# Batch 0's scores in two halves of the tokens, and the order of the transposes of the next batch's x

## The chip, the cores and the metric

The kernel runs on one core of a Trainium2 chip. The metric is the device time of one execution, in microseconds; lower is better.

## The reference, cut to what matters

```python
B, H, S, Ns, D = (8, 8, 512, 32, 64)          # x: B H S D, state: B H Ns D
# attention in both directions
scores  = scale * x @ state.T                  # per head, S x Ns
a       = softmax(scores)                      # over the 32 states
xread   = a @ state
scores2 = scale * state @ x.T                  # per head, Ns x S
a2      = softmax(scores2)                     # over the 512 tokens
sread   = a2 @ x
x2      = concat([xread, sread], axis=2)       # B H (512+32) D -> 4352 x 512
# two linear layers
h   = x2 @ w_in                                # 512 -> 2048
g   = h * sigmoid(1.702 * h)
out = g @ w_out                                # 2048 -> 512, float32
```

The two weights come as float64; the kernel reads their 32-bit words and puts float32 together itself.

## The kernel before, in words

Everything is written out by hand: there is no scheduler, and each engine runs its instructions in the order in which the program issues them. The kernel handles the 8 batches one after another. For a batch it transposes the state (`att_state`, L252, copied from PSUM by ScalarE at L254) and x in four pieces of two heads (`att_xT`, L262, copied at L263), forms the scores with the matmuls of `by_state` (L280), takes both softmaxes, multiplies the state into `w_in` (`att_M`, L280 again, copied at L391), and runs the up product on the attention weights and that product, then Gelu, then the down product with `w_out`. Batches 0 and 1 use plain matmuls (L462 up, L480 down). From batch 2 on the up product is a Strassen scheme (`up_strassen`, L891, additions on VectorE at L901, Gelus on ScalarE at L898) and the down product a two-level one (`strassen_two`, L646) with seven block products P1 to P7; P1, for one, consists of two halves of 16 matmul records, P1a and P1b. Behind each half stands a hook: a list of steps of the next batch, made by `hooks_next`, that is issued there. The first hook, P1a, begins with the last steps of the up product (`rest`: two products, their additions and Gelus).

PSUM tiles come from pools that hand out their buffers in turn; a tile waits until the buffer's previous tile has been read. `att_ps` draws from `psA` with two buffers (tag "att"), and holds the transposes; `psH` has two buffers as well (tag "h") and holds up products; `bank_o` are four fixed banks.

```python
psA = ctx.enter_context(tc.tile_pool(name="psA", bufs=2, space=bass.MemoryType.PSUM))
psH = ctx.enter_context(tc.tile_pool(name="psH", bufs=2, space=bass.MemoryType.PSUM))
```

At the start, weights arrive in pieces of 512 KB through SyncE's one DMA queue: the first piece of `w_in`, then the state and the four token chunks of batch 0's x, then three more pieces of `w_in`, then batch 1's. A piece is rounded in two steps. `round_a` makes a mask: one operation on VectorE (L189) and two on ScalarE (L194, L195). `round_b` needs that mask and takes four operations on VectorE (L204 to L207). `powers_to(n)` issues the masks of the pieces below n, `round_to(n, ahead)` rounds the pieces below n, with masks some pieces ahead.

Batch 0's x is transposed by chunk of 128 tokens as it arrives (`att_xT_arriving`, L272, copied at L273 by VectorE and ScalarE in turn). Then come in program order: the scores of batch 0 over all 512 tokens (`att_scores`), the mask of the second piece, the 32x32 transposes of the scores on VectorE (`att_blocks`, L293), maximum, subtraction and exponential (`att_x_exp`, L329 to L331), the rounding of the second piece, the rest of that softmax (`att_x_norm`, L338 to L343), then batch 1's state, x and scores, the rounding of pieces 3 and 4, and `att_M(0, 0)`, the first use of rounded weights. `keep_warm(n)` puts n bfloat16 matmuls on zeros (L122) into TensorE's queue; their results aren't used.

Of the kernel before, what the change touches and what calls it, by code (L numbers as in the profile page):

```python
# [10 lines left out]
FP32 = mybir.dt.float32  # L11
I32 = mybir.dt.int32
U32 = mybir.dt.uint32
AF = mybir.ActivationFunctionType
ALU = mybir.AluOpType
AX = mybir.AxisListType
# [4 lines left out]
def kernel(  # L21
# [30 lines left out]
    nc = tc.nc  # L52

    B, H, S, D = x.shape
    Ns = state.shape[2]
    DM = H * D
    DF = moe_w_in.shape[1]
    P = 128
    NPR = P // Ns
    NG = H // NPR  # L60
    NF = DF // P
    SCH = S // P
# [3 lines left out]
    NB = S // Ns  # L66
    HF, HN = NF // 2, DM // 2
    scale = float(1.0 / np.sqrt(D))
# [10 lines left out]
    apool = ctx.enter_context(tc.tile_pool(name="apool", bufs=1))  # L79
# [4 lines left out]
    psH = ctx.enter_context(tc.tile_pool(name="psH", bufs=2, space=bass.MemoryType.PSUM))  # L84
# [4 lines left out]
    def att_ps(shape, name):  # L89
        return psA.tile(shape, FP32, tag="att", name=name)  # L90
# [26 lines left out]
    bank_o = [psO.tile([P, FC], FP32, tag=f"o{i}", name=f"o_{i}") for i in range(4)]  # L117

    def keep_warm(n):
        ps = psH.tile([P, FC], FP32, tag="h", name="warm")  # L120
        for _ in range(n):
            nc.tensor.matmul(ps, zeros[:, :P], zeros, start=True, stop=True)  # L122
# [17 lines left out]
    def x_heads(b, c, j):  # L140
        return xn[b][:, c, NG * j : NG * (j + 1)].rearrange("q g d -> q (g d)")
# [33 lines left out]
    for i, v in enumerate((8.0 * most, 8.0 * (most - least))):  # L175
        t = konst.tile([P, 1], FP32, name=f"edge_{i}")
# [7 lines left out]
    def round_a(i):  # L184

        _, hi = words(i)
        sc = low[:, 2 + i % (AHEAD + 1)].bitcast(I32)
        power[i] = sc
        nc.vector.tensor_scalar(sc, hi, 0x7FF00000, None, ALU.bitwise_and)  # L189
        if PIECES[i][0] == "o":  # L190
            nc.vector.tensor_scalar(sc, sc, most, least, ALU.min, ALU.max)
            nc.vector.tensor_scalar(sc, sc, -least, 8.0, ALU.add, ALU.mult)
            return
        nc.scalar.activation(out=sc.bitcast(FP32), in_=sc, func=AF.Relu, bias=edge[0], scale=-8.0)  # L194
        nc.scalar.activation(out=sc, in_=sc.bitcast(FP32), func=AF.Relu, bias=edge[1], scale=-1.0)  # L195
# [21 lines left out]
    def load_weights(upto):  # L217
        while done["load"] < min(upto, len(PIECES)):
            load_weight(done["load"])
            done["load"] += 1  # L220

    def powers_to(n):
        while done["a"] < min(n, len(PIECES)):
            load_weights(done["a"] + 1)
            round_a(done["a"])
            done["a"] += 1
# [21 lines left out]
    A = {b: {} for b in range(B)}  # L248
# [4 lines left out]
        A[b]["stT"] = apool.tile([P, P], FP32, tag="stT", name=f"stT_{b}", bufs=2)  # L253
        nc.scalar.copy(A[b]["stT"], ps)  # L254

    def att_xT(b, j, spare=False):
        if j == 0:
            A[b]["xT"] = apool.tile([P, NPR, S], FP32, tag="xT", name=f"xT_{b}")
        name = f"xT_{b}_{j}"
        ps = psH.tile([P, SCH, P], FP32, tag="h", name=name) if spare else att_ps([P, SCH, P], name)  # L260
        for c in range(SCH):
            nc.tensor.transpose(ps[:, c], x_heads(b, c, j), ident)  # L262
        nc.scalar.copy(A[b]["xT"][:, j], ps.rearrange("p c q -> p (c q)"))  # L263

    def att_xT_arriving(b, warm):

        A[b]["xT"] = apool.tile([P, NPR, S], FP32, tag="xT", name=f"xT_{b}")
        for c in range(SCH):
            keep_warm(warm)
            ps = att_ps([P, NPR, P], f"xT_{b}_{c}")  # L270
            for j in range(NPR):
                nc.tensor.transpose(ps[:, j], x_heads(b, c, j), ident)  # L272
            (nc.scalar.copy if c % 2 else nc.vector.tensor_copy)(A[b]["xT"][:, :, P * c : P * (c + 1)], ps)  # L273

    def by_state(b, ps, rhs):

        for j in range(NPR):
            for g in range(NG):
                rows, st = slice(D * g, D * (g + 1)), slice(Ns * j, Ns * (j + 1))
                nc.tensor.matmul(ps[g][st], A[b]["stT"][rows, st], rhs(rows, j), start=True, stop=True)  # L280

    def att_scores(b):
        a = A[b]
        a["s"] = bank_o[:NG] if b == 0 else bank_o[NG:]
        by_state(b, a["s"], lambda rows, j: a["xT"][rows, j])

    def att_blocks(b):

        a = A[b]
        t = apool.tile([P, NG, NB, Ns], FP32, tag="e1", name=f"e1_{b}")  # L290
        a["e1"] = t
        for g in range(NG):
            nc.vector.transpose(t[:, g].rearrange("p i n -> p (i n)"), a["s"][g])  # L293
# [30 lines left out]
    def att_x_exp(b):  # L324

        a = A[b]
        t = a["e1"].rearrange("p g i n -> p (g i) n")
        mx = apool.tile([P, NS1], FP32, tag="mx", name=f"mx_{b}")
        nc.vector.reduce_max(out=mx, in_=t, axis=AX.X)  # L329
        nc.vector.tensor_tensor(out=t, in0=t, in1=mx.to_broadcast((P, NS1, Ns)), op=ALU.subtract)  # L330
        nc.scalar.activation(out=t, in_=t, func=AF.Exp, scale=scale)  # L331
# [410 lines left out]
    def hooks_next(b):  # L742

        h = {}

        def at(name, fn, *args):
            h.setdefault(name, []).append((fn, args))

        at("P1a", att_state, b)
        at("P1a", att_xT, b, 0)  # L750
        at("P1b", att_xT, b, 1)
        at("P1b", att_xT, b, 2)
        at("P1b", att_xT, b, 3, True)
        at("P2a", att_scores, b)
        at("P2a", att_M, b, 0)
        at("P2a", att_M, b, 1, True)
        at("P2a", att_blocks, b)
        at("P2a", att_s_max, b)
        at("P2a", att_s_exp, b)
        for g in range(NG):  # L760
            at("P2a", x_max, b, g)
            at("P2a", x_sub, b, g)
        at("P2a", x_exp, b)
        at("P2", att_s_norm, b)
        for name, fn, *args in (
            ("P6.1", x_sum, 0), ("P6.2", x_sum, 1), ("P6.3", x_inverse), ("P6.4", x_scale, 0), ("P6.6", x_scale, 1),
        ):
            at(name, fn, b, *args)
        for g in range(NG):
            at("P6", att_eT, b, g)  # L770
            at("P6", x_back, b, g)
        at("P4a", att_sread, b)
        at("P4a", att_M, b, 3, True)
        at("P4a", att_M, b, 2)
        steps = up_sums(b)
        for name, n in (("P4b", 5), ("P7.1", 2), ("P7.2", 1), ("P7.3", 1), ("P7.4", 1), ("P7.6", 1), ("P7", 1), ("P3a", 3)):
            for fn, args in steps[:n]:
                at(name, fn, *args)
            steps = steps[n:]
        assert not steps  # L780
        at("P3a", att_srT, b)
        return h


    def up_sums(b):

        a = A[b]

        def tt(out, x0, x1, op=ALU.subtract):
            nc.vector.tensor_tensor(out=out(), in0=x0(), in1=x1(), op=op)  # L790

        def rooms(step):
            if step == 0:
                t = apool.tile([P, NG, NB, Ns], FP32, tag="e1", name=f"ta_{b}").rearrange("p g i n -> p (g i n)")
                a["T"] = [t[:, QT * i : QT * (i + 1)] for i in range(4)]
            elif step == 1:
                t = apool.tile([P, NPR, S], FP32, tag="xT", name=f"ms_{b}")
                a["S1"], a["S2"] = t[:, :2], t[:, 2:]
            else:
                t = apool.tile([P, NG, SCH, P], FP32, tag="eT", name=f"m4_{b}")  # L800
                a["S4"] = t.rearrange("p g c q -> p g (c q)")

        def T(i):
            return lambda: a["T"][i]

        def R(g, i):
            return lambda: a["aT"][:, g, QT * i : QT * (i + 1)]

        def M(c, g):
            return lambda: a["M", c][:, g]  # L810

        def V(name, c):
            return lambda: a[name][:, c]

        steps = [(rooms, (0,))]
        steps += [(tt, v) for v in ((T(0), R(0, 1), R(0, 0)), (T(1), R(1, 1), T(0)), (T(2), R(1, 1), R(0, 1)), (T(3), R(1, 0), T(1)))]
        steps.append((rooms, (1,)))
        for c in range(2):
            steps.append((tt, (V("S1", c), M(2 + c, 0), M(2 + c, 1), ALU.add)))
            steps.append((tt, (V("S2", c), V("S1", c), M(c, 0))))  # L820
            steps.append((tt, (M(2 + c, 0), M(c, 0), M(2 + c, 0))))
        steps.append((rooms, (2,)))
        steps += [(tt, (V("S4", c), M(c, 1), V("S2", c))) for c in range(2)]
        return steps
# [137 lines left out]
    round_to(1, 0)  # L962
    att_state(0)
    att_xT_arriving(0, 2)
    att_scores(0)
    powers_to(2)
    att_blocks(0)
    att_x_exp(0)
    round_to(2, 1)
    att_x_norm(0)  # L970
    keep_warm(24)
# [2 lines left out]
        keep_warm(2)  # L974
        att_xT(1, j)
    att_scores(1)
    keep_warm(24)
    powers_to(4)
    round_to(NPR, 2)
    att_M(0, 0)  # L980
# [142 lines left out]
```

## Time and profile before

| | |
|---|---|
| median of 3 runs | 747.09 us (745.83, 747.09, 747.61) |
| the profiled execution: its own time, its span | 747.61 us, 745.8 us |
| mean granted TensorE clock | 0.996 |
| TensorE matmul busy | 732.2 us (98%) |
| VectorE, ScalarE busy | 501.9 us (67%), 231.6 us (31%) |
| first M of batch 0 on TensorE | at 29.16 us |
| time from batch to batch at the hook P1a (state transposes at 246.62, 326.71, 406.81) | 80.1 us |

The span goes from the first to the last instruction of the profiled execution. PE is TensorE's matmuls, PEld its weight loads, DVE VectorE, ACT ScalarE, SP the engine that issues the DMAs. A line of a timeline gives start and duration in us, the engine, the line of the kernel and the operation, out<-in with tile names, shape and number of instructions, and in brackets the idle time of the engine before it and what ended that. A matmul in float32 is recorded as two.

### The profile page before, as it was taken

How to read it: one execution, taken by the hardware profiler on the slowest of the kernel's cores; microseconds unless marked ns; L12 is line 12 of the kernel's file. 1: busy time of each engine (PE TensorE's matmuls, PEld its weight loads, DVE VectorE, ACT ScalarE, POOL GpSimd, SP SyncE). 2: the span in 40 equal slices, each digit the busy share in tenths (PEclk: the TensorE clock that was granted, in tenths of full speed). 3: DMA queues.
4: the chain of work that ended last, by engine and by line, in shares of the span. 5: the costliest groups of instructions: out<-in, count | busy, mean ns of one | idle time of the engine just before them, and what ended most of it. 6: DMA issues, size and time to landing. Idle time of an engine off the chain costs nothing.

```text
span 745.8 us, 10913 instructions
## 1 busy us (share of the span) xinstructions
PE 732.2 (98%) x4553; PEld 568.0 (76%) x4555; DVE 501.9 (67%) x947; ACT 231.6 (31%) x421; POOL 0.8 (0%) x8
## 2 busy tenths in 40 slices
PE   8989999999999999999999999999999999999996
PEld 3423444458788798888888789878888888899995
DVE  5999699705946776576756765677657774768340
ACT  4667610121424411443134421451143313300220
POOL 0000000000000000000000000000000000000000
PEclk9999999999999999999999999999999999999999
DMA  9811246010012000300040003100030001000000
GB/s 234 337 58 56 85 142 173 0 54 3 29 46 45 1 15 30 74 1 15 2 102 1 15 2 83 21 1 16 29 74 1 15 2 42 1 15 29 15 1 28
DMA packets 48768, 35.29 MB, mean 47 GB/s; under 512 B 36432, under 2 KB 44112, under 8 KB 48720
## 3 DMA queue, kind: packets, MB, share of 16 engines
q1 hardware_dynamic: 48720, 34.61, 16.2%
q8 instruction: 35, 0.57, 0.3%
q14 instruction: 13, 0.11, 0.0%
HBM read 25.69 MB, written 8.91 MB: 46 GB/s over the span
## 4 chain that ended last, share of the span: by engine, by line
PE 95%; SPq 2%; DMA 1%; ACT 1%; issue 0%; DVE 0%; DVEq 0%; ACTq 0%
PE o L646 28%; PE o L891 16%; PE o L523 9%; PE h L462 8%; PE o L480 7%; PE low L598 6%; PE upx L891 6%; PE o L598 4%; PE M L280 4%; PE xT L262 2%; SPq L138 1%; PE sr L411 1%; PE o L280 1%; PE upx_sr L891 1%; DMA out_dram<-osb_sr 1%; PE warm L122 1%
## 5 line engine op out<-in xcount | busy, mean ns | idle before, releaser
L901 DVE TENSOR_TENSOR g<-o,g 128x512 f32<-128x512 f32 (+1 forms) x140 | 88.1, 651 | 87.4 <-PE o L891 86.3
L646 PE MATMUL o<-w_out,g 128*128 128x256 f32 x576 | 130.0, 380 | 0.0
L646 PEld LDWEIGHTS o<-w_out,g 128*128 128x128 f32 x576 | 107.4, 190 | 18.1 <-issue 4.2
L898 ACT ACTIVATE g<-g 128x512 f32<-128x512 f32 (+1 forms) x84 | 49.8, 599 | 100.5 <-DVE g L901 100.5
L891 PE MATMUL upx<-aT,M 128*128 128x256 f32 x192 | 49.3, 379 | 0.0
L891 PE MATMUL o<-ta,M 128*128 128x256 f32 x192 | 49.3, 379 | 0.0
L891 PE MATMUL o<-ta,ms 128*128 128x256 f32 x192 | 48.4, 380 | 0.0
L391 ACT COPY M<-M 128x512 f32<-128x512 f32 x64 | 33.2, 596 | 42.3 <-PE M L280 42.3
L646 PE MATMUL o<-sums,g 128*128 128x256 f32 x192 | 43.8, 382 | 0.0
L523 PE MATMUL o<-w_out,g 128*128 128x256 f32 x192 | 42.9, 380 | 0.0
L646 PE MATMUL o<-sums,later 128*128 128x256 f32 x192 | 42.4, 379 | 0.0
L646 PEld LDWEIGHTS o<-sums,g 128*128 128x128 f32 x192 | 35.6, 190 | 8.6 <-issue 4.2
L523 PEld LDWEIGHTS o<-w_out,g 128*128 128x128 f32 x192 | 36.1, 190 | 6.0 <-issue 1.3
L891 PEld LDWEIGHTS o<-ta,ms 128*128 128x128 f32 x192 | 36.4, 190 | 5.2 <-DVE osb L542 0.3
L891 PEld LDWEIGHTS upx<-aT,M 128*128 128x128 f32 x192 | 36.5, 190 | 5.0
L646 PEld LDWEIGHTS o<-sums,later 128*128 128x128 f32 x192 | 36.5, 190 | 5.0
L891 PEld LDWEIGHTS o<-ta,M 128*128 128x128 f32 x192 | 36.5, 190 | 5.0
L503 DVE TENSOR_TENSOR later<-g,g 128x512 f32<-128x512 f32 (+1 forms) x32 | 20.8, 650 | 21.5 <-ACT g L465 21.5
L462 PE MATMUL h<-low,M 128*128 128x512 f32 x64 | 31.5, 630 | 2.1 <-ACT M L391 2.1
L280 PE MATMUL M<-w_in,stT 64*32 64x512 f32 x512 | 33.2, 594 | 0.2 <-ACT eT L401 0.2
L462 PE MATMUL h<-aT,M 128*128 128x512 f32 x64 | 28.7, 599 | 2.3 <-ACT M L391 2.3
L601 DVE TENSOR_TENSOR pu<-low,pu 128x128 f32<-128x128 f32 x12 | 3.5, 291 | 39.6 <-PE low L598 39.6
(172 smaller groups left out, 1135.5 us busy)
## 6 DMA issues: line engine op xcount, KB each, us to landing
later<-in_moe_w_out_dram SPq DMA_DIRECT2D x16, 512.0 KB
xn<-in_x_dram SPq DMA_DIRECT2D x28, 256.0 KB
w_out<-in_moe_w_in_dram SPq DMA_DIRECT2D x12, 512.0 KB
out_dram<-osb SPq DMA_DIRECT2D x20, 256.0 KB
out_dram<-later SPq DMA_DIRECT2D x12, 256.0 KB
later<-in_moe_w_in_dram SPq DMA_DIRECT2D x4, 512.0 KB
sums<-in_x_dram SPq DMA_DIRECT2D x4, 256.0 KB
stn<-in_state_dram SPq DMA_DIRECT2D x16, 32.0 KB
```

The costliest lines, as they stand in the source:

```text
L262: nc.tensor.transpose(ps[:, c], x_heads(b, c, j), ident)
L280: nc.tensor.matmul(ps[g][st], A[b]["stT"][rows, st], rhs(rows, j), start=True, stop=True)
L391: nc.scalar.copy(m[:, g], ps[g])
L462: nc.tensor.matmul(hps, lhs[i], rhs[i], start=(i == 0), stop=(i == n - 1))
L480: nc.tensor.matmul(ops, G[key, f // 2][:, f % 2, P * r : P * (r + 1)], w_out[:, f], start=(f == 0), stop=(f == NF - 1))
L503: nc.vector.tensor_tensor(out=s1, in0=a21, in1=a22, op=ALU.add)
L523: nc.tensor.matmul(ps[:, r], lhs[f][:, P * r : P * (r + 1)], rhs[:, f], start=(first and r == 0 and f == 0), stop=(f == HF - 1), skip_grou ...
L598: nc.tensor.matmul(ps, lhs[f], rhs[:, f], start=(f == 0), stop=(f == QF - 1))
L646: nc.tensor.matmul(ps[:, r], lhs[f][:, P * r : P * (r + 1)], rhs[:, f], start=(r == 0 and f == 0), stop=(f == HF - 1), skip_group_check=True,)
L891: nc.tensor.matmul(ps[:, k], lhs[i][:, o : o + P], rhs[i], start=(first and k == 0 and i == 0), stop=(i == n - 1), skip_group_check=True,)
L898: nc.scalar.activation(out=dst, in_=src, func=AF.Gelu_apprx_sigmoid)
L901: nc.vector.tensor_tensor(out=dst, in0=ps, in1=x, op=ALU.add)
```

## The change

1. Batch 0's x: the copies of chunks 1, 2 and 3 are ScalarE's, that of chunk 0 VectorE's. The two warming matmuls before chunks 2 and 3 are gone.
2. A new function, `att_half`, forms the scores of 256 tokens, transposes them in 32x32 blocks, and takes their maximum and the difference. It is called behind chunk 1 and behind chunk 3; the first half's scores lie in `psH`, the second's in two banks of `bank_o`. The mask of the second weight piece is issued behind the first half. The exponential over all tokens comes after both, and `att_scores(0)`, whose scores now serve the other softmax alone, after that. `att_blocks(0)` and `att_x_exp(0)` fall away.
3. The 24 warming matmuls ahead of the rounding of pieces 3 and 4 become 14.
4. For batches 3 to 7, `att_xT` of piece 1 is issued in the hook P1a in place of P1b, and that of piece 3 takes its PSUM tile from `psA` in place of `psH`.

```diff
-    def att_xT(b, j, spare=False):
+    def att_xT(b, j):
...
-        name = f"xT_{b}_{j}"
-        ps = psH.tile([P, SCH, P], FP32, tag="h", name=name) if spare else att_ps([P, SCH, P], name)
+        ps = att_ps([P, SCH, P], f"xT_{b}_{j}")
...
         for c in range(SCH):
-            keep_warm(warm)
+            if c < 2:
+                keep_warm(warm)
...
-            (nc.scalar.copy if c % 2 else nc.vector.tensor_copy)(A[b]["xT"][:, :, P * c : P * (c + 1)], ps)
+            (nc.scalar.copy if c else nc.vector.tensor_copy)(A[b]["xT"][:, :, P * c : P * (c + 1)], ps)
+            if c % 2:
+                att_half(b, c // 2)
+            if c == 1:
+                powers_to(2)
...
+    def att_half(b, i):
+
+        a = A[b]
+        if i == 0:
+            a["e1"] = apool.tile([P, NG, NB, Ns], FP32, tag="e1", name=f"e1_{b}")
+            a["mx"] = apool.tile([P, NG, NB], FP32, tag="mx", name=f"mx_{b}")
+        n, w = S // 2, slice(NB // 2 * i, NB // 2 * (i + 1))
+        ps = [v[:, :n] for v in bank_o[NG:]] if i else [psH.tile([P, n], FP32, tag="h", name=f"sh_{b}_{g}") for g in range(NG)]
+        by_state(b, ps, lambda rows, j: a["xT"][rows, j, n * i : n * (i + 1)])
+        for g in range(NG):
+            nc.vector.transpose(a["e1"][:, g, w].rearrange("p i n -> p (i n)"), ps[g])
+        t, mx = a["e1"][:, :, w], a["mx"][:, :, w]
+        nc.vector.reduce_max(out=mx, in_=t, axis=AX.X)
+        nc.vector.tensor_tensor(out=t, in0=t, in1=mx.to_broadcast((P, NG, NB // 2, Ns)), op=ALU.subtract)
...
         at("P1a", att_xT, b, 0)
-        at("P1b", att_xT, b, 1)
+        at("P1a", att_xT, b, 1)
         at("P1b", att_xT, b, 2)
-        at("P1b", att_xT, b, 3, True)
+        at("P1b", att_xT, b, 3)
...
     att_xT_arriving(0, 2)
+    nc.scalar.activation(out=A[0]["e1"], in_=A[0]["e1"], func=AF.Exp, scale=scale)
     att_scores(0)
     powers_to(2)
-    att_blocks(0)
-    att_x_exp(0)
     round_to(2, 1)
...
     att_scores(1)
-    keep_warm(24)
+    keep_warm(14)
     powers_to(4)
```

## The prediction

> **What bounds the kernel now.** I read the page's chain first, then TensorE's list of waits, then the timeline at the two places that the diff touches (the first 32 us, and the seam where one batch's up product meets the next batch's transposes), then the clock in narrow windows. The page says that the end is set by TensorE almost alone:
>
> ```profile
> PE 732.2 (98%) x4553; PEld 568.0 (76%) x4555; DVE 501.9 (67%) x947; ACT 231.6 (31%) x421; POOL 0.8 (0%) x8
> ...
> PE 95%; SPq 2%; DMA 1%; ACT 1%; issue 0%; DVE 0%; DVEq 0%; ACTq 0%
> ```
>
> The waits (us in total, times, longest) are few, and all lie in the first 103 us:
>
> ```profile
> PE h L462 <- ACT M L391: 4.4, 3, 2.1
> ...
> PE o L280 <- ACT xT L273: 0.7, 1, 0.7
> ```
>
> So from about 103 us on TensorE has no idle time that an edit could recover, and any wait put into its queue there moves the end by its full length.
>
> The seam, as it stands for batch 3 (start, duration, engine, line):
>
> ```profile
> 246.62 0.27 PE L252 MATMUL stT<-ident,stn 128*128 128x128 f32 x1
> ...
> 246.72 0.60 PE L262 MATMUL xT<-ident,xn 128*128 128x128 f32 x4
> ...
> 247.16 3.62 PE L646 MATMUL o<-w_out,g 128*128 128x256 f32 x16
> ...
> 247.54 0.63 ACT L898 ACTIVATE g<-g 128x512 f32<-128x512 f32 x1 [0.23 <-DVE g L901]
> 248.08 0.24 ACT L254 COPY stT<-stT 128x128 f32<-128x128 f32 x1
> ...
> 250.62 1.47 PE L262 MATMUL xT<-ident,xn 128*128 128x128 f32 x12
> 251.25 1.56 ACT L263 COPY xT<-xT 128x512 f32<-128x512 f32 x3 [2.44 <-PE xT L262]
> ```
>
> To be seen: the state's transpose ends at 246.9, but its copy out of PSUM runs only at 248.08 to 248.32, since ScalarE has two Gelus of the last up tiles ahead of it, the second held by VectorE's addition. TensorE doesn't notice: it goes from piece 0's transposes straight to the next 16 matmuls at 247.16.
>
> The start:
>
> ```profile
> 9.95 0.69 DVE L273 COPY xT<-xT 128x512 f32<-128x512 f32 x1 [0.42 <-PE xT L272]
> ...
> 11.49 1.09 PE L280 MATMUL o<-xT,stT 64*32 64x512 f32 x16 [0.68 <-ACT xT L273]
> 12.21 0.43 DVE L189 TENSOR_SCALAR low<-w_out 128x512 int32<-128x512 int32 x1 [1.56 <-DMA w_out<-in_moe_w_in_dram]
> ...
> 12.67 0.72 ACT L194 ACTIVATE low<-low,edge 128x512 f32<-128x512 int32 x1 [1.24 <-DVE low L189]
> 13.43 0.72 ACT L195 ACTIVATE low<-low,edge 128x512 int32<-128x512 f32 x1
> ...
> 16.41 0.42 DVE L189 TENSOR_SCALAR low<-w_out 128x512 int32<-128x512 int32 x1
> ```
>
> The second weight piece lands at 12.2 us; its mask occupies VectorE to 12.64 and ScalarE to 14.15. From 12.2 on VectorE is never idle until 56.9. M of batch 0, the first use of rounded weights, starts on TensorE at 29.16; its last weight piece is rounded at 28.90, and the 24 warming matmuls before it are done at 29.1: both limits are met at once.
>
> The clock (span, then the busy times, then the granted clock and the DMA):
>
> ```profile
> 43.00:43.30 0.30, 0.30 (x2) 0.18 (x1) 0.30 (x2) 0.00 (x0) 0.00 (x0) 1.00 0.09 27
> ...
> 44.00:45.00 1.00, 1.00 (x2) 0.34 (x1) 0.96 (x2) 0.46 (x1) 0.00 (x0) 0.50 0.00 0
> ...
> 47.00:47.50 0.50, 0.50 (x2) 0.22 (x2) 0.47 (x2) 0.04 (x1) 0.00 (x0) 1.00 0.00 0
> ```
>
> After TensorE's 2.12 us wait at 39.91 the granted clock falls to 0.50 from about 43.4 to 46.8, 3.4 us, which costs half of that, 1.7 us (those 16 matmuls took 8.83 us, the same ones at 31.00 took 7.13). The 1.50 us wait at 51.88 brought no fall.
>
> **The seam, five times (batches 3 to 7).** The transposes of piece 1 move from behind the second half of P1 to right behind those of piece 0, and piece 3 goes to the two-buffer pool instead of the other one. That pool hands out its two buffers in turn: state, piece 0, then piece 1 gets the state's buffer. So piece 1's first transpose waits for the state's copy, which ends at 248.32. A released matmul starts 0.05 us later (at 9.26 after a copy that ended at 9.21), so it starts at 248.37 where TensorE now goes on at 247.16: 1.21 us of idle time. Behind the waiting transpose stand the 16 matmuls of P1's second half, and they can't pass it (at 9.75 the warming matmuls followed the held transposes in order). The same rows of the other four batches (copy at 328.18, 408.27, 488.37, 568.47; next matmuls at 327.26, 407.36, 487.45, 567.55) give the same difference within 0.01. The four transposes themselves cost 0.44 us in either place. Pieces 2 and 3 find their buffers copied (by 248.8 and about 249.9, needed at 252). TensorE had no wait later in the batch that this could relieve, and the scores at 255.48 keep their distance from the last copy. Sum: 5 x 1.21 = **6.05 us**. Bounds: 0 if the buffer is free earlier, 5 x 1.70 = 8.5 if the release came only with piece 0's copy (248.81); I take 6.05, the row of the buffer itself. A 1.2 us gap is below the 1.50 that left the clock alone.
>
> [...]
>
> **The start, step by step.** Half 0: its copies are done at 9.53; eight matmuls of 256 columns take about half of the 1.09, say 0.6 (1.09 at most), so 10.2. VectorE then needs two 256-wide transposes (half of the 1.31: 0.7), a maximum (0.68, row of 128x512) and a subtraction (0.69): 12.25. That is just where the mask of the second piece stands today, so half 0 is hidden in the 1.56 us of idle time and the removed xT copy. But now the mask stands *ahead* of the copies of chunks 2 and 3 on ScalarE, and both copies are ScalarE's. They can't start before the mask's second step lets them, 14.1, and end at 15.2 (two copies take 1.08 elsewhere). Half 1 on TensorE: 15.25 to 15.8. VectorE again 0.7 + 0.68 + 0.69 and gaps: the next mask at 17.9, where it is 16.41 now. VectorE thus loses 3.2 us idle (12.7 to 15.85) and gains 1.9 done early: **about 1.5 us late**, and the rounding of piece 3 ends at 28.90 + 1.46 = 30.36. The exponential (18.0 to 19.1) is ready before VectorE's sum at 20.5, which still covers it.
>
> TensorE: scores of batch 0 for the other softmax are now extra work (1.09, from 15.75), then 24 warming matmuls from 16.8 (5.19 from first to next, rows 12.51 and 17.70): state of batch 1 at 22.0 (17.70 now). Then the rows of today: 3.7 to the last transposes, scores to 27.4, 14 warming matmuls (0.22 each, 3.1): M at 30.45. The ten removed ones (2.2 us) and the four removed between the chunks are thus not a gain: they only keep the later start from being worse. ScalarE's masks of pieces 3 and 4 stand behind batch 1's copies, end of the first at 27.7, needed at 28.35: just in time. So M is 30.45 - 29.16 = **1.3 us later with the clock at 1.00**.
>
> But TensorE now sits idle from about 11.3 to 15.25, 3.9 us without warming matmuls. The 2.12 us gap brought a fall, 1.50 didn't; 3.9 very likely does. Half clock for 3.4 us costs up to 1.7 us of what follows (less where part of it passes in the idle time), average about 1.3, and nothing covers it: M at 31.8, and VectorE's piece 3 at about 31.1, since batch 1's copies and the mask behind them come late too. Startup: +1.3 (warm) to +3.0 (a full fall), taken **+2.6**. [...]
>
> From 31 us on TensorE leads (VectorE's last input for batch 1 comes at 39.88 and is used at 42.03, 2.1 us of slack for its 1.5 us), so the startup's shift goes through to the end. The later 2.12 us gap lies between a fall and none (the 1.50 us gap had none), so shifted in time its fall, 1.7 us in the profiled run, may vanish: 0 to -1.7, I take -0.4.
>
> **Sum.** The profiled execution took 747.61 (span 745.8 and 1.8 around it), 0.52 above the median of 747.09. From it: 747.61 + 6.05 + 2.6 - 0.4 = 755.9; the median of runs stands half a microsecond lower, so **755.4 us**. With this case's own bounds: 747.1 + 6.05 + 1.3 - 1.7 - 0.9 (half the spread of the runs, 745.83 to 747.61) = 751.8, and 747.1 + 8.5 + 2.6 - 0.4 = 757.8.
>
> **The rivals.**
> - *The clock stays up in the gap.* Startup +1.3: 747.1 + 6.05 + 1.3 = 754.4. For it: the 1.50 us gap brought no fall, so gaps are not punished by their length alone. Against: the 2.12 us row. Chance 0.2.
> - *The half clock lasts twice as long* (6.8 us) and drags piece 3's mask along: 1.3 + 3.4 = 4.7 instead of 2.6, so 757.8 with nothing won back. For it: the gap is longer than the 3.4 us that one fall lasted. Chance 0.1.
> - *The seam doesn't stall*: the state's buffer is free by 247.16. Against it stand five copies at 1.2 us after that point. Only the start counts: 747.1 + 2.2 = 749.3. Chance 0.07.
> - *Faster: the halves fill VectorE's wait.* If chunks 2 and 3 were copied before the mask (piece 1 landing after about 12.2 but its mask not holding ScalarE), half of the 3.8 us from 12.67 to 16.41 would be done early: -1.9, or 745.2. It decides the sign only where the seam's stall is under 0.4 us a batch (1.9 / 5); the rows say 1.21. Chance 0.05.
>
> The forecast has 0.58. A measurement of this kernel tells about 0.3% (2.2 us) from no change: under 744.9 is faster, over 749.3 slower. Faster 0.05; same 0.03, the lower half of the no-stall case; slower 0.92. The range holds the forecast's bounds and the first two rivals, and leaves out the last two: 751.5 to 758.0.
>
> **What would show it.** In the profile after: five waits of TensorE's xT transposes for ScalarE's state copy, 1.2 us each, 6 in total; the period from batch to batch 81.3 us in place of 80.1; batch 0's second half of scores starting at about 15.2, behind ScalarE's second mask and two copies; M of batch 0 at 30.4 to 32.2; a granted clock of 0.50 somewhere from 13 to 20 us. I am wrong if the period stays at 80.1, or if M starts before 29.2.

## The result and the profile after

The changed kernel takes 756.91 us (median of 4 runs, 756.16 to 757.40); the kernel before, beside it, 747.35 us. The ratio is 1.0128, 95% interval 1.0108 to 1.0149: slower by 9.6 us, where 8.3 had been forecast, within the range of 751.5 to 758.0. The median lies 1.5 us above the forecast's 755.4 and 0.9 us below the 757.8 of the second rival. The profiled execution took 756.98 us with a span of 755.2; the one of before 747.61 and 745.8.

Busy time and the clock by slices, from the page of the changed kernel:

```profile
PE 731.3 (97%) x4571; PEld 566.9 (75%) x4573; DVE 501.7 (66%) x950; ACT 232.3 (31%) x422; POOL 0.8 (0%) x8
...
PEclk8999999999999999999999999999999999999999
```

TensorE is busy as long as before (731.3 us to 732.2), in a span that is 9.4 us longer: TensorE waits longer, and the clock is lower in the first slice. The list of TensorE's waits (us in total, times, longest) names the places. The first and the last row are new, the third was 0.7 us before:

```profile
PE xT L261 <- ACT stT L254: 5.3, 5, 1.1
PE h L481 <- ACT M L410: 4.4, 3, 2.1
PE o L284 <- ACT xT L273: 4.1, 1, 4.1
PE sh L284 <- DVE xT L273: 1.2, 1, 1.2
```

**The seam.** The timeline at the same place as before, batch 3 (start, duration, engine, line and operation, in brackets the idle time before it):

```profile
249.33 0.27 PE L252 MATMUL stT<-ident,stn 128*128 128x128 f32 x1
...
249.44 0.60 PE L261 MATMUL xT<-ident,xn 128*128 128x128 f32 x4
...
250.25 0.63 ACT L917 ACTIVATE g<-g 128x512 f32<-128x512 f32 x1 [0.23 <-DVE g L920]
250.79 0.25 ACT L254 COPY stT<-stT 128x128 f32<-128x128 f32 x1
...
251.09 0.66 PE L261 MATMUL xT<-ident,xn 128*128 128x128 f32 x4 [1.05 <-ACT stT L254]
...
251.58 3.62 PE L665 MATMUL o<-w_out,g 128*128 128x256 f32 x16
```

ScalarE's copy of the state ends at 251.04, and piece 1's transposes start at 251.09. Up to the state's transpose the two kernels lie 2.71 us apart (249.33 and 246.62), and ScalarE's copy stands where it stood relative to it; the 16 matmuls behind lie 4.42 us apart (251.58 and 247.16). Of the 1.71 us that came in between, 0.44 are the four transposes that moved here, and 1.27 us a batch are the wait. The batch-to-batch period says the same: state transposes at 330.70 and 412.07, 81.37 us, in place of 80.10.

**The start**, with the mask of the second weight piece, the second half's scores and the first M:

```profile
9.74 0.67 PE L284 MATMUL sh<-xT,stT 64*32 64x256 f32 x16 [1.19 <-DVE xT L273]
...
12.63 0.42 DVE L189 TENSOR_SCALAR low<-w_out 128x512 int32<-128x512 int32 x1
13.09 0.72 ACT L194 ACTIVATE low<-low,edge 128x512 f32<-128x512 int32 x1 [3.91 <-DVE low L189]
13.84 0.72 ACT L195 ACTIVATE low<-low,edge 128x512 int32<-128x512 f32 x1
14.47 1.05 ACT L273 COPY xT<-xT 128x512 f32<-128x512 f32 x2
15.57 2.81 PE L284 MATMUL o<-xT,stT 64*32 64x256 f32 x32 [4.14 <-ACT xT L273]
...
18.91 0.42 DVE L189 TENSOR_SCALAR low<-w_out 128x512 int32<-128x512 int32 x1
...
30.80 0.69 DVE L205 SCALAR_TENSOR_TENSOR low<-w_out,low 128x512 int32<-128x512 int32 x1 [1.33 <-ACT low L195]
...
33.55 1.09 PE L284 MATMUL M<-w_in,stT 64*32 64x512 f32 x16
```

ScalarE runs the mask first and the two copies after it, as forecast; TensorE sits idle for 4.14 us. The M matmuls start at 33.55 in place of 29.16: 4.4 us late. The clock in the stretches between (span, then busy times, then the granted clock and the DMA):

```profile
14.00:15.00 1.00, 0.00 (x0) 0.00 (x0) 0.00 (x0) 1.00 (x3) 0.00 (x0) 0.80 0.77 162
15.00:16.00 1.00, 0.43 (x8) 0.23 (x16) 0.00 (x0) 0.52 (x2) 0.00 (x0) 0.50 1.06 229
...
20.00:21.00 1.00, 1.00 (x4) 0.45 (x3) 0.97 (x3) 0.97 (x3) 0.00 (x0) 0.50 0.99 377
21.00:22.00 1.00, 1.00 (x5) 0.36 (x4) 1.00 (x2) 0.46 (x1) 0.00 (x0) 0.79 1.02 360
22.00:23.00 1.00, 1.00 (x6) 0.49 (x5) 0.93 (x3) 0.00 (x0) 0.00 (x0) 1.00 0.99 406
```

The mixed windows give the edges: at 0.80, 0.4 us of the window were at half clock. So the half clock lasts from 14.6 to 21.4, 6.8 us. At 46.43, in this execution, the 16 matmuls behind the 2.12 us wait now run at the full clock (1.00 from 46 to 54):

```profile
46.43 7.13 PE L481 MATMUL h<-low,M 128*128 128x512 f32 x16 [2.12 <-ACT M L410]
53.49 1.09 PE L284 MATMUL M<-w_in,stT 64*32 64x512 f32 x16
```

They took 8.83 us before, so the lag shrinks from 4.40 us (46.43 against 42.03) to 2.70 (53.49 against 50.79), and stays there to the first seam (2.71 at 249.33). The ledger of the two profiled executions: 4.4 - 1.7 + 5 x 1.27 = 9.05; the last down product starts 9.08 us later (745.51 against 736.43), and the remaining 0.3 of the spans' 9.4 lies behind it.

### The profile page after: what moved, and what is told of

The parts are those of the page before. It is cut to its first block, busy times and chain, and to the rows that moved or that the text cites. A ratio compares the mean times of both kernels' runs of the same rounds, so it can differ in the third digit from the quotient of the medians.

```text
span 755.2 us, 10952 instructions
## 1 busy us (share of the span) xinstructions
PE 731.3 (97%) x4571; PEld 566.9 (75%) x4573; DVE 501.7 (66%) x950; ACT 232.3 (31%) x422; POOL 0.8 (0%) x8
## 4 chain that ended last, share of the span: by engine, by line
PE 94%; ACT 2%; DMA 1%; DVE 1%; issue 0%; DVEq 0%; ACTq 0%
PE o L665 28%; PE o L910 16%; PE o L542 9%; PE h L481 8%; PE o L499 7%; PE low L617 6%; PE upx L910 5%; PE o L617 4%; PE M L284 4%; PE warm L122 2%; PE xT L261 1%; PE o L284 1%; PE sr L430 1%; PE upx_sr L910 1%; DMA out_dram<-osb_sr 1%; PE eT L419 1%
## 5 line engine op out<-in xcount | busy, mean ns | idle before, releaser
L522 DVE TENSOR_TENSOR later<-g,g 128x512 f32<-128x512 f32 (+1 forms) x32 | 20.8, 650 | 21.6 <-ACT g L484 21.6
L481 PE MATMUL h<-low,M 128*128 128x512 f32 x64 | 29.8, 600 | 2.1 <-ACT M L410 2.1
```

The source lines that it names most:

```text
L481: nc.tensor.matmul(hps, lhs[i], rhs[i], start=(i == 0), stop=(i == n - 1))
L522: nc.vector.tensor_tensor(out=s1, in0=a21, in1=a22, op=ALU.add)
```

## The experiments

All times are medians, and each program was profiled in one execution; the kernel before measured 747.9 us (12 runs) beside the first four and 746.9 us (29 runs, 745.79 to 748.52) beside the last four. Each kernel starts from the changed one or the one before, as its expectation says.

**The hooks undone** (e1).

```diff
...
-        at("P1a", att_xT, b, 1)
+        at("P1b", att_xT, b, 1)
         at("P1b", att_xT, b, 2)
-        at("P1b", att_xT, b, 3)
+        at("P1b", att_xT, b, 3, True)
```

> The changed kernel with the hooks P1a and P1b as before: only the start is changed. Theory (seam and start add up, each with its own cause): the seam's 5 x 1.27 = 6.4 us go, the start's +2.7 us stay: 756.9 - 6.4 = 750.5 us, period 80.1 us, no wait of TensorE for the state's copy. Rival (the seam's stall is partly a consequence of the late start, or swallows time that would be lost elsewhere): between 751.5 and 755, with new waits on TensorE after 100 us.

Measured 750.55 us, ratio to the kernel before 1.0037 (1.0024 to 1.0051). The five waits are gone and the period is 80.10 us (state transposes at 249.01, 329.10, 409.20). 6.4 us of the change's loss belong to the hooks, 2.6 to the start; the two come to 9.0 of the 9.6, since the kernel before lay at 747.9 here and at 747.35 beside the changed one.

**The new hooks alone** (e2).

```diff
-        at("P1b", att_xT, b, 1)
+        at("P1a", att_xT, b, 1)
         at("P1b", att_xT, b, 2)
-        at("P1b", att_xT, b, 3, True)
+        at("P1b", att_xT, b, 3)
```

> The kernel before with the new order of the hooks alone: piece 1 in P1a, piece 3 in the two-buffer pool. Theory: +6.4 us, 747.3 + 6.4 = 753.7 us, five waits of 1.05 us and a period of 81.37 us, the start as before (M at 29.2). Rival (stall depends on the changed start): under 750 us.

Measured 753.63 us, ratio 1.0086 (1.0068 to 1.0104), 5.7 us above the kernel before; five waits and a period of 81.37 us (245.01, 326.38, 407.75) as expected. The loss is there whatever the start is; that the medians differ by 5.7 and the periods by 5 x 1.27 = 6.35 lies within the spread of the runs (746.0 to 749.1 for the kernel before), of which e4 to e7 tell more. One of the six runs took 757.13 us, 2.6 us more than the next, at a mean granted clock of 0.993; it has no profile, and its cause stays open. In the profiled execution the 2.12 us wait, in the same start as before, brought no fall of the clock (1.00 from 40 to 64):

```profile
42.12 7.13 PE L462 MATMUL h<-low,M 128*128 128x512 f32 x16 [2.12 <-ACT M L391]
```

**Another pool for the state's transpose** (e3).

```diff
...
-        ps = att_ps([P, P], f"stT_{b}")
+        ps = psH.tile([P, P], FP32, tag="h", name=name) if spare else att_ps([P, P], name)
...
-        at("P1a", att_state, b)
+        at("P1a", att_state, b, True)
```

> The changed kernel, with the state's transpose of batches 3 to 7 in the other pool, so that piece 1 gets a buffer that nobody has to copy first; piece 1 stays in P1a. Theory (the stall is the wait for the state's buffer, not the place of piece 1): the five waits vanish, period 80.1 us, 756.9 - 6.4 = 750.5 us. Rival (the place costs: ScalarE's Gelus and copies of P1a collide with two pieces at once): the wait moves to another copy, about 1 us a batch stays, 754 to 757 us.

Measured 750.65 us, ratio 1.0039 (1.0026 to 1.0053), the same as with the hooks undone. The timeline at the seam, with piece 1 still in P1a:

```profile
249.69 0.27 PE L253 MATMUL stT<-ident,stn 128*128 128x128 f32 x1
...
249.79 1.04 PE L262 MATMUL xT<-ident,xn 128*128 128x128 f32 x8
...
250.67 3.62 PE L666 MATMUL o<-w_out,g 128*128 128x256 f32 x16
...
251.15 0.25 ACT L255 COPY stT<-stT 128x128 f32<-128x128 f32 x1
```

Eight transposes run in one go, and the matmuls follow while the state's copy is still to come. So the place of piece 1 costs nothing; the shared buffer costs all of it. The place brings nothing either.

**A delay alone** (e4).

```diff
     att_scores(1)
-    keep_warm(24)
+    keep_warm(44)
```

> The kernel before with 44 warming matmuls in place of 24 ahead of the first M: TensorE is 20 x 0.2165 = 4.3 us late there, as in the changed kernel, and nothing else differs. Theory (the start's +4.4 us at M became +2.7 at the end because the fall of the clock behind the 2.12 us gap, 1.7 us, does not occur at the shifted place): 747.3 + 4.3 - 1.7 = 749.9 us in runs that resemble the profiled one, with a clock of 1.00 at 46 to 52 us. Rival (the 1.7 us come from something else in the changed start, or the fall occurs wherever the gap lies): 747.3 + 4.3 = 751.6 us, clock 0.50 for 3.4 us after the gap.

Measured 751.62 us, the rival's figure, ratio 1.0051 (1.0036 to 1.0065); the six runs lie in two groups, 750.0 to 751.0 and 752.2 to 752.6. In the profiled one (752.37) the M is 4.7 us late and the clock falls behind the wait all the same:

```profile
46.75 8.83 PE L462 MATMUL h<-low,M 128*128 128x512 f32 x16 [2.12 <-ACT M L391]
```

The theory fell in this point: the place alone doesn't decide on the fall (here the clock is at 0.50 from 48.0 to 51.4). A better one is that it comes in some executions and not in others, as the profiles of the kernel before and of e2 already show; the next runs test that.

**The idle stretch filled** (e5; hooks as before, as in all that follow from the changed kernel).

```diff
                 nc.tensor.transpose(ps[:, j], x_heads(b, c, j), ident)
+            if c == 3:
+                keep_warm(17)
             (nc.scalar.copy if c else nc.vector.tensor_copy)(...)
```

> The changed start alone (hooks as before), with 17 warming matmuls (3.7 us) put into TensorE's idle stretch between the last transposes of batch 0's x and the second half of the scores. Theory (of the start's 4.4 us at the first M, about 3 are the half clock that follows the idle stretch, and 1.3 to 1.5 the mask ahead of ScalarE's copies): clock 1.00 from 10 to 40 us, M at 30.4 to 30.8, time 747.9 + 1.4 = 749.3 us, and a spread as wide as that of the kernel before. Rival (the clock costs nothing, the extra matmuls and VectorE's wait set the start): M at 33 as without them, 750.6 us.

Measured 749.35 us, ratio 1.0024 (1.0014 to 1.0033): 2.4 us above the kernel beside it, where 1.4 had been expected. The half clock is gone (1.00 in every window from 10 to 52 us) and the same stretch is shorter:

```profile
15.36 1.52 PE L287 MATMUL o<-xT,stT 64*32 64x256 f32 x32 [0.47 <-ACT xT L276]
16.81 5.35 PE L122 MATMUL warm<-sums 128*128 128x512 bf16 x24
...
30.53 1.30 PE L287 MATMUL M<-w_in,stT 64*32 64x512 f32 x16
```

M starts at 30.53, 1.4 us later than before: this is what the new start costs with the clock up, the mask's place, the halves and the scores done twice taken together. The remaining 3.0 us of the changed kernel's 4.4 at M are the clock's. The medians don't show them whole, since the runs lie in two groups: five took 747.62 to 747.77, 2.8 us less than e1's median, and seven 749.31 to 749.62, at a lower granted clock (0.995 to 0.997, in place of 0.998 to 1.0). The profiled one is of the five and has no later fall; that the seven have it is the author's estimate from their clock and from the distance of 1.8 us.

**The mask behind the copies** (e6).

```diff
+            if c == 3:
+                powers_to(2)
             if c % 2:
                 att_half(b, c // 2)
-            if c == 1:
-                powers_to(2)
```

> The changed start alone (hooks as before), with the mask of the second weight piece issued behind ScalarE's copies of chunks 2 and 3 and ahead of the second half's scores. Theory (the mask's place, not the halves, is what costs): the second half's scores start at about 12.2 instead of 15.5, no long idle stretch, clock 1.00 until 40 us, VectorE reaches batch 0's sum at about 17.8 (19.02 in the kernel before), M at 27.4 to 28.0: 747.9 - 1.4 = 746.5 us. Rival (the halves cost by themselves, by 0.1 us more for each half-wide operation and 1.1 us of scores done twice): M at 29.2 or later, 748 us or more.

Measured 746.13 us, ratio 0.9987 (0.9977 to 0.9997): 0.8 us below the kernel beside it, where 1.4 had been expected. ScalarE's queue now has the copies first:

```profile
10.81 1.07 ACT L274 COPY xT<-xT 128x512 f32<-128x512 f32 x2 [1.50 <-PE xT L273]
...
12.86 0.72 ACT L194 ACTIVATE low<-low,edge 128x512 f32<-128x512 int32 x1 [0.98 <-DVE low L189]
...
17.48 1.21 DVE L358 TENSOR_REDUCE sm<-e 128x32 f32<-128x1024 f32 x1
```

The second half's scores start at 11.93, VectorE reaches its sum 1.5 us earlier than in the kernel before (17.48 against 19.02), and M starts at 27.15, 2.0 us earlier. The halves do what their cut suggests, once nothing stands ahead of their copies. The twelve runs fall into 744.3 to 744.6 (four) and 745.9 to 746.9 (eight), 1.8 us apart: close to the 1.70 us that one fall cost (8.83 us in place of 7.13), and the slower ones again show the lower granted clock (0.995 to 0.997, in place of 0.997 and 0.998). With eight of twelve in the slower group, against 13 of the 29 of the kernel before, the median gains less than the groups do: their spans are 1.2 to 1.6 us shorter than the same group's before (742.65 against 744.2, 744.5 against 745.7).

**The later wait filled** (e7).

```diff
     att_M(1, 0)
+    keep_warm(9)
```

> The kernel before with 9 warming matmuls (1.95 us) in TensorE's 2.12 us wait for the copies of batch 1's first M. Theory (the fall of the clock behind this wait, 1.7 us, comes in some executions and not in others, and that makes up half of the spread of the kernel before): no execution has it, the median falls by about 1 us to 746.9 and the spread of 3.1 us shrinks to under 2. Rival (the clock's fall depends on something else, or the warming matmuls delay what follows): median 747.9 or later.

Measured 746.04 us, ratio 0.9989 (0.9981 to 0.9998); nine of eleven runs within 745.89 to 746.19, the highest 747.08, against 745.79 to 748.52 for the kernel before. The matmuls still start at 42.00, now at the full clock (1.00 from 42 to 52):

```profile
39.81 2.12 PE L122 MATMUL warm<-sums 128*128 128x512 bf16 x9
42.00 7.13 PE L462 MATMUL h<-low,M 128*128 128x512 f32 x16
```

**Both** (e8): the edits of e6 and e7 on the changed kernel with its old hooks.

> The last two together: the halves with the mask behind the copies, the hooks as before, and 9 warming matmuls in the later wait. Theory (the two effects are separate and add): 747.9 - 1.4 - 1.0 = 745.5 us. Rival (the earlier start only meets VectorE or the weights' arrival later and gives its gain back): about 747 us.

Measured 744.51 us (744.37 to 744.96), ratio 0.9969 (0.9958 to 0.9981). The upper group of e6 is gone. This version beats both kernels: by 2.4 us the one before, by some 12 the changed one (756.91, not measured beside it). The gain is the sum of the two that had been expected, 1.4 and 1.0; the time is lower than 745.5 because the kernel before is.

## Why the prediction was right, point by point

The profiled execution is 1.1 us above the 755.9 of the sum: 0.3 from the seam, 0.5 from the start, and 0.3 behind the last down product. The median lies 0.07 us below that execution, where 0.5 had been put.

- **The seam: right in cause and place, 0.06 us a batch short.** Five waits for the state's buffer, 1.27 us each in the period where 1.21 stood in the sum, so 6.35 in place of 6.05. The difference is that four transposes that start from a standstill take 0.49 us until the next matmul (251.09 to 251.58), where 0.44 was put. The list of waits shows 1.05 us each, not the 1.2 that had been named, since it counts from the recorded end of piece 0's transposes (250.04); counted from where the next matmul would have started (0.44 us after 249.44), the wait is 1.21. E2 shows the loss without the rest, E3 that the buffer is its cause.
- **The mask ahead of ScalarE's copies: right.** The second half's scores were put at 15.25 and came at 15.57; the start with the clock up was put at 1.3 us at M and measures 1.4 (e5). VectorE's next mask was put at 17.9 and came at 18.91: about 0.45 us of this since half 1 ran at half clock (VectorE follows its start by 1.20 us, by 0.75 in e5), 0.3 since its scores started later, and the rest since half 1 takes 0.75 us even at full clock, not 0.55, and two half-wide transposes 0.78 us, not 0.7.
- **"Half clock for 3.4 us": the term that was mis-sized.** It lasted 6.8 us in the profiled execution. That was the second rival, with a chance of 0.1: 4.7 us at M in its price, 4.4 measured. With the clock up the step costs 1.4 (e5), so the clock's term is 3.0 where 1.3 stood. The profile of e3 shows the shorter kind, 0.50 from about 15.5 to 18.9 and M at 32.23, so both occur. By the same term the sign "M at 30.4 to 32.2" was missed: M came at 33.55.
- **"Just in time" for the mask of piece 3: wrong.** VectorE waits 1.33 us for it at 30.80, since batch 1's copies were late behind the slow warming matmuls. It cost nothing: the piece is rounded at 32.82, before TensorE has finished warming.
- **The later fall: right in direction, too small.** -0.4 in the sum, -1.7 in the profiled pair. That rival's "nothing won back" therefore didn't come, and the start's net is +2.7 in the profiles and +2.6 by e1, where 2.2 was put. Against the executions of the kernel before whose granted clock was 0.998 to 1.0, the new start costs about 4.3 (spans of e1 748.4 to 749.1, of those 744.2 to 744.7). The two errors of the clock nearly cancelled, and in the three profiles with this start they go together: the changed kernel and e1 have 6.8 us of half clock early and no later fall, e3 has 3.4 us early and 3.4 later (46.2 to 49.6), and 14 of the 15 runs of these three have the same mean granted clock, 0.993. The prediction treated the two as separate; that its sum for the start came so close is luck.
- **The faster rival** put the gain of the halves at 1.9 us if the mask didn't hold ScalarE; e6 has M 2.0 us earlier, of which 1.2 to 1.6 reach the end. It was right in its price, and its condition wasn't met by this change.

## What to carry to other kernels

Before a transpose or any other PSUM tile is moved forward on a full TensorE, find which tile had its buffer last, and when the engine that empties it gets there: a two-buffer pool turned a free move into 1.27 us a batch. Work put between two halves of a chain can stand ahead of the second half on an engine that both use; here the mask's two ScalarE steps (13.09 and 13.84, the copies at 14.47), not the halves, cost the start. And fill waits of TensorE like the two here, since where the clock fell behind them it cost most of the wait again: 1.7 us behind 2.12, 3.0 at M behind 4.14.

## What the runs showed of the hardware that was not expected

One idle stretch of 4.14 us was followed by 6.8 us at half clock, although TensorE was at work again after the first microsecond of it (14.6 to 21.4, the matmuls from 15.57; 14.0 to 20.8 in e1). In e3, with the same start, it was 3.4 us (15.5 to 18.9), and there the later wait brought a fall as well:

```profile
45.10 8.83 PE L482 MATMUL h<-low,M 128*128 128x512 f32 x16 [2.12 <-ACT M L411]
...
46.00:48.00 2.00, 2.00 (x4) 0.89 (x3) 1.93 (x4) 0.11 (x1) 0.00 (x0) 0.54 0.03 8
48.00:50.00 2.00, 2.00 (x4) 0.74 (x3) 1.97 (x5) 1.82 (x3) 0.00 (x0) 0.60 0.00 0
```

Of the falls read from these traces behind the two waits, four last 3.4 us (43.39 to 46.80 in the kernel before, the two of e3, 48.0 to 51.4 in e4) and two 6.8 us (the changed kernel, e1). Behind the same 2.12 us wait the clock fell in three profiles (the kernel before, e3, e4) and was at 1.00 in five (the changed kernel, e1, e2, e5, e6). The 1.50 us wait at 51.88 in the kernel before brought no fall (1.00 from 52 to 56). What decides between a fall and none, and between 3.4 and 6.8 us, was not shown.

That the 2.12 us wait brings the fall in some executions of one program and not in others is the author's estimate from the granted clocks: e5 has five runs at 747.62 to 747.77 (0.998 to 1.0) and seven at 749.31 to 749.62 (0.995 to 0.997), 1.8 us apart; with nine matmuls on zeros in the wait, nine of eleven runs lie within 0.3 us (e7).
